# VectorE's small steps taken by turns, seven more pairs of exps for it, and weights loaded at other times, in a fused attention and state-space kernel

## The chip, the cores and the metric

The kernel runs on one core of one Trainium2 chip. The metric is the device time of one execution in microseconds (us), the median of several runs. The core's engines work side by side: TensorE (PE; its weight loads are shown apart as PEld), VectorE (DVE), ScalarE (ACT), GpSimd (POOL), and SyncE (SP), whose queue issues nearly all DMAs here.

## The reference

```python
x = A_x                                         # 1 x 2048 x 1024
g = sigmoid((x * gate_w).sum(-1, keepdims=True))
# a: a diagonal complex state-space model (SSM) of 1024 states over 2048 steps
dt = exp(log_dt); Lam_bar = exp(dt * Lam)
B_bar = ((Lam_bar - 1.0) / Lam)[:, None] * Bmat
Bu = einsum("bld,pd->blp", x + 0j, B_bar)
for t in range(L): h = Lam_bar[None, :] * h + Bu[:, t, :]
a = 2.0 * einsum("blp,dp->bld", hseq, Cmat).real + x * Dskip
# b: attention, 32 heads of 32
q, k, v = (x @ wqkv).reshape(B, S, 3, H, Dh).transpose(2, 0, 3, 1, 4)
p = softmax(einsum("bhqd,bhkd->bhqk", q, k) * Dh ** -0.5)
b = (p @ v).transpose(0, 2, 1, 3).reshape(B, S, D) @ wo
out = g * a + (1 - g) * b
```

## The kernel before

The attention is the frame. Its 32 heads form 8 groups of 4 heads; a group has 8 units (256 queries each), and a unit has 8 bursts (256 keys each): 512 bursts, numbered `p`. In a burst, `burst` puts 8 score matmuls on TensorE (four heads side by side), and two exps, `exp(0)` and `exp(1)`, each over 128 x 1024 scores, turn them into bf16 tiles of `f_pt` (in the first 60 bursts also into other tiles that are still free). Line 1643 is a full exp. One burst later, `pv` (line 1709) multiplies these tiles with V into PSUM bank 6. After a unit, `normalize` takes reciprocals (line 1722) and scales (1723), and a transposing DMA (1729) writes the result to `f_OT`.

**Exps on VectorE.** In chosen bursts one of ScalarE's two exps is short (128 x 768, line 1640): the other 256 columns, one head, are VectorE's. It reads the scores and scales them to integers (line 1633, `x_in`), and for a pair of such bursts runs three steps of a cubic (lines 1667, 1668, 1664, all on the tile `f_xq`); GpSimd then makes bf16 bits of it (1665), and TensorE takes them at line 1688 (`x_pv`), by the end of the unit. `exp(1)` of such a burst waits until `x_in` has read. `X_PLAN` lists the bursts at which a pair starts: a unit has none, one or two. There are 92 pairs.

**Dense work.** Beside the attention, TensorE takes four 512-column matmuls of dense work in a burst, in chains that all gather in PSUM bank 7: the K, V and Q projections of the next group (lines 1426, 1445), the SSM's input u (1457), its output c (1504, with the skip at 1510) and the output projection (1535). The build loop chooses the chains: c if its items are done, otherwise u, otherwise projections, which are forced when the bursts left in the group are few (`left <= need + 4`, where `need` is twice the number of projection chains left). The output chains run last, with ready times from burst 442 on.

**VectorE's background work.** u goes through DRAM (stored at line 1462, reloaded to `f_ub` at 1474) and comes back as 32 *items*, each eleven or so steps: four products with tables, two sums, two scans (1362), two sums to `hp`. Tables and folds of C (`bg2`) are further steps. The loop builds each burst's instruction list with a clock of its own: it adds up the costs written beside each step (`I_MM`, `X_LAST` and others), and fills each burst up to a limit. The steps of exps (`xbg`) come first, then items (`bg`), then `bg2`. Every engine runs its list in order; if a step is later than planned, everything behind it on that engine is late.

**Loads.** B's rows come by transposing DMAs into three slots (1076), C's by `ld_c` (1081) from burst `C_LOADS` = 28, one pair every fourth burst. Projection weights (`ld_w`, line 1071): Q's has one slot, K's and V's two each, so that the weights of group g + 2 are asked for at burst 25 of group g, and Q's of g + 1 at burst 28. The output weights come in five DMAs: two rows at burst 386, six when the c chains are done and later.

**Ending.** For the last unit (queries 1792 to 2047) the output's sums over the first seven groups are made ahead (`part`, `sum7`); two of the four are split in a high and a low bf16 half (lines 1553, 1554) and put into PSUM by four matmuls (`preload`, line 1975) before the last values. After them come the last reciprocal (1984), the scaling (1987), a transpose on TensorE (1990) and four matmuls (2002).

Of the kernel before, what the change touches and what calls it, by code (L numbers as in the profile page):

```python
# [932 lines left out]
C_LOADS = 28  # L933

X_AT = ((0, 2), (4, 6), (0, 4))
X_PLAN = (64, 72, 80, 88, 92, 96, 100, 104, 108, 112, 116, 120, 124, 128, 132, 136, 144, 152, 160, 168, 172, 176, 180, 184, 188, 192, 200, 208, 216, 224, 228, 232, 236, 240, 244, 248, 252, 256, 260, 264, 272, 280, 288, 296, 304, 312, 316, 320, 324, 328, 332, 336, 344, 352, 356, 360, 364, 368, 372, 376, 380, 384, 388, 392, 396, 400, 404, 408, 412, 416, 420, 424, 428, 432, 436, 440, 444, 448, 452, 456, 460, 464, 468, 472, 476, 480, 484, 488, 492, 496, 500, 504)
X_COLS = 256
F_TS, F_ST = 1.32, 1.24
I_MM = 0.61
X_LAST = 0.735  # L940
# [18 lines left out]
class FastPath:  # L959

    def __init__(self, nc, S, es, d, flag):
# [11 lines left out]
        wb = T("wb", [128, 8192], BF)  # L973
        self.wq = wb[:, 0:1024].rearrange("p (a n) -> p a n", a=8)
        self.wkv = wb[:, 1024:5120].rearrange("p (s q a n) -> p s q a n", s=2, q=2, a=8)
        self.bT = wb[:, 5120:8192].rearrange("p (s a n) -> p s a n", s=3, a=8)

        row = lambda o, n: wb[:, o:o + 1024 * n].rearrange("p (a n) -> p a n", a=n)
        self.wo3 = [row(1024, 2), row(5120, 3), row(3072, 1), self.cT[0][:, 0:1, :], self.cT[0][:, 1:2, :]]
        self.wo = [(self.wo3[0][:, a, :], "wo0") for a in range(2)] + [(self.wo3[4][:, 0, :], "wo4")] + [(self.wo3[1][:, a, :], "wo1") for a in range(3)]  # L980
        self.wo += [(self.wo3[3][:, 0, :], "wo3"), (self.wo3[2][:, 0, :], "wo2")]
# [5 lines left out]
        self.hpx = wb[:, 5120:8192].rearrange("p (k n) -> p k n", k=6)  # L987
# [77 lines left out]
    def w_of(self, g, part):  # L1065
        return (self.wkv[:, g % 2, part - 1], ("w", g % 2, part)) if part else (self.wq, ("w", 0, 0))
# [275 lines left out]
    def item_ops(self, j, ch, n):  # L1342
# [9 lines left out]
        def tt(c, o, a, b, op, r, w):  # L1352
            ops.append((c, lambda: dve(lambda e: e.tensor_tensor(o, a, b, op), r, w)))
# [3 lines left out]
        ops.append((0.0, lambda: self.used_u(n)))  # L1357
        tt(0.63, ut[:, 0, :], t[0], t[3], ALU.add, [k[0], k[3]], [("ut", 0)])
# [5 lines left out]
        if ch < 3:  # L1364
            ops.append((0.0, lambda: self.pool(lambda e: e.tensor_copy(self.hl[:, :, j], ht[:, :, 511]), [("ht", 0), ("ht", 1)], [("hl", j)])))
# [368 lines left out]
    def build(self):  # L1734
# [10 lines left out]
        for part in (1, 2):  # L1745
            self.ld_w(1, part)
# [389 lines left out]
```

## Time and profile before

| | |
|---|---|
| median of 3 runs (lowest, highest) | 929.36 us (927.99, 930.2) |
| the profiled execution | 928.11 us |
| its span, first to last instruction | 926.3 us |
| ScalarE busy | 907.3 us (98%) |
| TensorE busy | 902.5 us (97%) |
| VectorE busy | 758.4 us (82%) |
| GpSimd busy | 86.8 us (9%) |
| granted TensorE clock, mean | 0.996 |

Busy times are of one execution. Matmuls are pipelined and their ends modelled, so that TensorE's share says little; its waits say more. Consecutive VectorE and ScalarE instructions overlap a little, so that the distance from start to start, not the busy time of one, is what one costs. The profile also has a timeline, a table of busy time by stage, the waits, and the chain of work that ended last.

### The profile page before, as it was taken

What the parts mean: (1) busy time and instruction counts of PE and PEld (TensorE: products, weight loads), DVE (VectorE), ACT (ScalarE), POOL (GpSimd) and SP (SyncE); (2) the same over time, 40 slices, a digit from 0 to 9 for tenths busy, and PEclk for the clock granted to TensorE, in tenths of its full rate; (3) what the DMA queues carried; (4) which work ended last, traced back from release to release, by engine and by line L of the source; (5) the groups of instructions that cost most, each with busy time, mean ns of one, the idle gap of its engine ahead of it and who ended that gap; (6) DMA issues with size and microseconds to landing.
All of it is one profiled execution on the core that took longest, in us unless ns stands there. A gap on an engine that the chain in (4) does not pass through costs nothing.

```text
span 926.3 us, 33979 instructions
## 1 busy us (share of the span) xinstructions
PE 902.5 (97%) x15316; PEld 503.9 (54%) x15316; DVE 758.4 (82%) x1310; ACT 907.3 (98%) x1034; POOL 86.8 (9%) x156
## 2 busy tenths in 40 slices
PE   8899999999999999999999999999999999999996
PEld 4554754557555565546655565555655655445553
DVE  2788989998989999989989999899988655776665
ACT  6999999999999999999999999999999999999996
POOL 2000000111000101011111020000010010001010
PEclk9999999999999999999999999999999999999998
DMA  9569747750457101272012511413001112424312
GB/s 195 87 116 184 93 84 138 144 116 5 81 113 152 50 20 49 67 147 53 19 51 65 126 45 31 104 63 103 20 15 43 31 51 77 156 83 128 114 62 75
DMA packets 170934, 77.69 MB, mean 84 GB/s; under 512 B 147232, under 2 KB 155424, under 8 KB 170784
## 3 DMA queue, kind: packets, MB, share of 16 engines
q1 hardware_dynamic: 168624, 74.94, 36.3%
q8 instruction: 121, 1.98, 0.9%
q10 hardware_dynamic: 2160, 0.53, 0.3%
q14 instruction: 29, 0.24, 0.1%
HBM read 25.18 MB, written 20.97 MB: 50 GB/s over the span
## 4 chain that ended last, share of the span: by engine, by line
PE 52%; ACT 40%; DVE 4%; DMA 2%; SPq 1%; issue 1%; POOL 0%; DVEq 0%; ACTq 0%
ACT f_pt L1643 32%; PE f_ps L1709 14%; PE f_ps L1624 10%; PE f_ps L1426 9%; PE f_ps L1504 7%; PE f_ps L1457 6%; ACT f_pt L1640 5%; PE f_ps L1445 5%; SPq L1062 1%; ACT f_cT L1643 1%; PE f_ps L1688 1%; DMA f_xT<-in_A_x_dram 1%; ACT f_Et L1643 1%; DMA f_wb<-in_A_B_im_dram 1%; DMA f_ub<-u_scratch 0%
## 5 line engine op out<-in xcount | busy, mean ns | idle before, releaser
L1643 ACT ACTIVATE f_pt<-f_ps 128x1024 bf16<-128x1024 f32 x760 | 728.8, 1090 | 1.5 <-PE f_ps L1624 1.3
L1709 PEld LDWEIGHTS f_ps<-f_V,f_pt 128*128 128x128 bf16 x7184 | 222.2, 96 | 95.3 <-issue 68.7
L1709 PE MATMUL f_ps<-f_V,f_pt 128*128 128x33 bf16 x7184 | 258.0, 178 | 0.0
L1624 PE MATMUL f_ps<-f_Q,f_K 32*128 32x256 bf16 x4096 | 203.3, 273 | 10.8 <-ACT f_pt L1643 3.3
L1640 ACT ACTIVATE f_pt<-f_ps 128x768 bf16<-128x768 f32 x184 | 165.3, 898 | 0.7 <-PE f_ps L1624 0.6
L1624 PEld LDWEIGHTS f_ps<-f_Q,f_K 32*128 32x128 bf16 x4096 | 60.7, 92 | 148.0 <-ACT f_pt L1643 120.6
L1457 PE MATMUL f_ps<-f_xT,f_wb 128*128 128x512 bf16 x512 | 131.5, 379 | 1.6 <-DMA f_wb<-in_A_B_im_dram 0.7
L1665 POOL TENSOR_SCALAR f_xp<-f_xq 128x512 int16<-128x512 f32 x92 | 67.3, 732 | 646.0 <-DVE f_xq L1664 471.3
L1426 PE MATMUL f_ps<-f_xT,f_wb 128*128 128x512 bf16 x464 | 119.3, 379 | 0.1
L1633 DVE TENSOR_SCALAR f_xi<-f_ps 128x256 int32<-128x256 f32 x184 | 77.4, 421 | 17.6 <-PE f_ps L1624 13.3
L1362 DVE TENSOR_TENSOR_SCAN f_ht<-f_pf,f_init,f_ut 128x512 bf16<-128x512 f32 x64 | 81.3, 1279 | 0.0
L1504 PE MATMUL f_ps<-f_cT,f_hp 128*128 128x512 bf16 x272 | 74.5, 379 | 0.1
L1667 DVE SCALAR_TENSOR_TENSOR f_xq<-f_xi 128x512 f32<-128x512 uint16 x92 | 63.7, 692 | 3.2
L1668 DVE SCALAR_TENSOR_TENSOR f_xq<-f_xq,f_xi 128x512 f32<-128x512 f32 x92 | 63.6, 692 | 3.1
L1664 DVE SCALAR_TENSOR_TENSOR f_xq<-f_xi,f_xq 128x512 f32<-128x512 int16 x92 | 63.5, 690 | 2.6
L1457 PEld LDWEIGHTS f_ps<-f_xT,f_wb 128*128 128x128 bf16 x512 | 40.1, 96 | 40.5 <-issue 8.6
L1535 PE MATMUL f_ps<-f_wb,f_OT 128*128 128x512 bf16 x188 | 61.2, 381 | 0.4 <-DVE f_Et L1547 0.4
L1445 PE MATMUL f_ps<-f_wb,f_xT 128*128 128x128 bf16 x896 | 59.3, 219 | 0.0
L1426 PEld LDWEIGHTS f_ps<-f_xT,f_wb 128*128 128x128 bf16 x464 | 36.1, 96 | 35.6 <-issue 7.6
L1461 DVE CAST f_ub<-f_ps 128x512 bf16<-128x512 f32 x64 | 44.1, 688 | 10.4 <-PE f_ps L1457 9.7
L1445 PEld LDWEIGHTS f_ps<-f_wb,f_xT 128*128 128x128 bf16 x896 | 50.4, 97 | 3.8 <-issue 3.8
L1722 DVE RECIPROCAL f_rc<-f_ps 128x8 f32<-128x8 f32 x63 | 13.1, 207 | 47.6 <-PE f_ps L1688 43.5
(149 smaller groups left out, 822.5 us busy)
## 6 DMA issues: line engine op xcount, KB each, us to landing
u_scratch<-f_ub SPq DMA_DIRECT2D x64, 128.0 KB, 2.1
f_ub<-u_scratch SPq DMA_DIRECT2D x32, 256.0 KB, 3.0
ag_scratch<-f_Ag SPq DMA_DIRECT2D x32, 256.0 KB, 2.0
f_hp<-ag_scratch SPq DMA_DIRECT2D x32, 256.0 KB, 3.0
f_wb<-in_B_wqkv_dram SPq DMA_DIRECT2D x21, 256.0 KB, 4.1
out_dram<-f_xT SPq DMA_DIRECT2D x16, 256.0 KB, 2.2
f_OT<-f_On SPq DMA_TRANSPOSE x63, 2.3
f_wb<-in_B_wo_dram SPq DMA_DIRECT2D x1, 768.0 KB
```

The costliest lines, as they stand in the source:

```text
L1362: ops.append((1.24, lambda ri=ri: dve(lambda e: e.tensor_tensor_scan(ht[:, ri, :], rr, ut[:, ri, :], self.init[:, ri, j:j + 1], ALU.mult, ...
L1426: mms.append((1, lambda e, f, l, a=a, w=w: e.matmul(ps[:, bank, :], w[:, a, :], xT[:, a, 512 * ch:512 * (ch + 1)], start=f, stop=l), [tok] ...
L1445: m = e.matmul(ps[:, bank, 128 * q:128 * (q + 1)], xT[:, a, 128 * kt:128 * (kt + 1)], w[:, a, :], start=(a == 0), stop=(a == 7))
L1457: mms.append((1, lambda e, f, l, a=a: e.matmul(ps[:, 7, :], bT[:, (2 * n + ri) % 3, a, :], xT[:, a, 512 * ch:512 * (ch + 1)], start=f, sto ...
L1504: mms.append((1, lambda e, f, l, j=j, ri=ri, h=h: e.matmul(ps[:, 7, :], h[:, cols], cT[ri][:, j, 512 * cb:512 * (cb + 1)], start=f, stop=l ...
L1624: m = e.matmul(ps[:, 2 * sl[h // 2] + h % 2, 256 * kl:256 * (kl + 1)], K[32 * h:32 * h + 32, g % 2, 128 * kt:128 * (kt + 1)], Q[32 * h:32 ...
L1633: first = self.dve(lambda e: e.tensor_scalar(self.xi[:, b % 2, X_COLS * n:X_COLS * (n + 1)], ps[:, 2 * s + 1, 512 - X_COLS:512], X_A, X_LO ...
L1640: self.S.op("act", lambda e: e.activation(flat(self.tile[p]), flat(ps[:, 2 * s:2 * s + 2, :]), ACT.Exp, scale=SCALE), reads=[("S", s)], wr ...
L1643: self.act(lambda e: e.activation(self.tile[p], ps[:, 2 * s:2 * s + 2, :], ACT.Exp, scale=SCALE), [("S", s)], [("pt", p)], "exp")
L1665: self.pool(lambda e: e.tensor_scalar(bits, xq[:], X_K, 128.0 * (E0 + 126.0), ALU.mult, ALU.add), ["xq"], p2, "x_p")
L1667: return [(0.73, 0.0, lambda: self.dve(lambda e: e.scalar_tensor_tensor(xq[:], lo, E2 / E3 * w, lo, ALU.add, ALU.mult), i2, ["xq"], "x_q") ...
L1709: m = e.matmul(ps[:, 6, o:o + 33], self.tile[p][:, h2, 256 * kl + 128 * qt:256 * kl + 128 * (qt + 1)], V[:, g % 2, 2 * i + kl, h, :], star ...
```

## The change

It does the following.

- The background steps carry a second cost, `DEP` = 0.12, counted only if the step follows one of its own kind (*lane*: x for exps, b for items, t for `bg2`). A function `mixed` gives the time of a set of steps taken by turns, and the first lane; the loop puts out one step of that lane and chooses again. The costs themselves are lower.
- `X_PLAN` has seven more entries, 268, 276, 284, 292, 300, 308 and 348: 99 pairs.
- Q's, K's and V's weights have one slot each. K's and V's of the next group are asked for at burst 0 of a group (K's of group 1 at burst 17, V's at the start), Q's at burst 38; the projections may start four bursts after. `C_LOADS` is 32.
- The output weights lie elsewhere and come as eight loads of one row: seven when the c chains are done, the last as before.
- The two steps that split the last sums go to `bg2`. Two of the four preloads come after the last values.

```diff
-C_LOADS = 28
+C_LOADS = 32
+W_AT = (38, 0, 17)
...
-I_MM = 0.61
-X_LAST = 0.735
+DEP = 0.12
+I_MM = 0.6
+X_LAST = 0.615
...
-        tt(0.63, ut[:, 0, :], t[0], t[3], ALU.add, [k[0], k[3]], [("ut", 0)])
-        tt(0.63, ut[:, 1, :], t[1], t[2], ALU.subtract, k[1:3], [("ut", 1)])
+        tt(0.61, ut[:, 0, :], t[0], t[3], ALU.add, [k[0], k[3]], [("ut", 0)], DEP)
+        tt(0.61, ut[:, 1, :], t[1], t[2], ALU.subtract, k[1:3], [("ut", 1)])
...
-                    self.dve(lambda e: e.tensor_copy(hi, su), [("sum7", i)], [("hi", i)])
-                    self.dve(lambda e: e.tensor_tensor(lo, su, hi, ALU.subtract), [("sum7", i), ("hi", i)], [("lo", i)])
+                    self.bg2 += [(0.34, lambda: self.dve(lambda e: e.tensor_copy(hi, su), [("sum7", i)], [("hi", i)])),
+                                 (0.72, lambda: self.dve(lambda e: e.tensor_tensor(lo, su, hi, ALU.subtract), [("sum7", i), ("hi", i)], [("lo", i)]))]
...
+    def mixed(self, xs, bs, ts):
+
+        rest = {"x": list(xs), "b": list(bs), "t": list(ts)}
+        t, lane, lead = 0.0, self.lane, ""
+        while True:
+            some = [s for s in "xbt" if rest[s]]
+            if not some:
+                return t, lead
+            s = next((s for s in some if s != lane), some[0])
+            if rest["b"] and rest["b"][0][0] == 0.0:
+                s = "b"
+            c, d = rest[s].pop(0)
+            lead = lead or s
+            if c > 0:
+                t += c + (d if s == lane else 0.0)
+                lane = s
...
-            if pg == 25 and g + 2 < GROUPS:
-                assert g or not (proj[0] or cur and cur.tag == "proj")
-                for part in (1, 2):
-                    self.ld_w(g + 2, part)
-            if pg == 28 and g + 1 < GROUPS:
-                assert not (cur and cur.tag == "proj")
+            if pg == W_AT[1 if g else 2] and g + 1 < GROUPS:
+                self.ld_w(g + 1, 1)
+                if g:
+                    self.ld_w(g + 1, 2)
+            if pg == W_AT[0] and g + 1 < GROUPS:
+                assert not proj[0]
                 self.ld_w(g + 1, 0)
...
                         for k in range(len(ts) + 1):
-                            u = used_t + sum(ts[:k])
+                            u, lead = self.mixed(xs[:i], bs[:j], ts[:k])
                             if u > room:
                                 break
-                            v = (u + (0.3 * i if ended is not None else 9.0 * i) + 0.05 * sum(bs[:j]), i, j, k)
+                            v = (u + (0.3 * i if ended is not None else 9.0 * i) + 0.05 * sum(x[0] for x in bs[:j]), i, j, k, lead)
...
-        preload()
-        self.pv(4 * NBURST - 4, 4 * NBURST)
+        preload(0)
+        self.pv(4 * NBURST - 4, 4 * NBURST - 2)
+        self.pv(4 * NBURST - 2, 4 * NBURST)
+        preload(1)
```

More of the change, by code (lines that the diff above doesn't have):

```diff
@@ L1806, in build @@
                 if n == 1:
-                    self.xbg += [[c, wait, f] for c, wait, f in self.x_ops(b)]
+                    self.xbg += self.x_ops(b)
+                self.lane = "x"
             q0, q1 = self.quarters[p]
@@ L1838, in build @@
+            if pg == W_AT[0] and g + 1 < GROUPS:
+                assert not proj[0]
                 self.ld_w(g + 1, 0)
             wsv = self.d["B_wo"].rearrange("(a p) n -> p a n", p=128)
-            if p == 386:
-                self.dma(lambda e: e.dma_start(self.wo3[0], wsv[:, 0:2, :]), [], ["wo0"] + [("w", 0, q) for q in (1, 2)], "ld_wo")
-            if not cs and cur is None and not wo1 and self.c_left[3] == 0:
+            if not wo1 and not cs and cur is None and self.c_left[3] == 0:
```

127 lines of the change are left out of this document (64 added, 63 removed).

## Prediction

> **What bounds the kernel now.** I read the page's head first, then ScalarE's waits, then the chain that ended last, then single stretches by the timeline and the table by stage.
>
> ```profile
> span 926.3 us, 33979 instructions
> PE 902.5 (97%) x15316; PEld 503.9 (54%) x15316; DVE 758.4 (82%) x1310; ACT 907.3 (98%) x1034; POOL 86.8 (9%) x156
> ACT f_pt L1643 <- PE f_ps L1624: 1.3, 4, 0.6
> ```
>
> ScalarE is busy for 907.3 of 926.3 us, and its longest sum of waits for scores in the ring of f_pt is 1.3 us. So the exps set the pace almost everywhere, and a change can win in three ways only: fewer columns for ScalarE, fewer of its few stalls, a shorter ending. The profiled execution took 928.11 us, 1.81 over its span; the median of the runs shown is 929.36, or 1.25 above that execution. I make the sum on 928.11 and add the 1.25 at the end.
>
> The chain of waits shows the two paces of ScalarE, for four bursts with one of their eight exps short, and for two bursts with one of four short:
>
> ```profile
> 541.36 6.42 ACT f_pt L1643 x7
> 548.48 6.42 ACT f_pt L1643 x7
> ...
> 839.06 2.75 ACT f_pt L1643 x3
> 842.51 2.75 ACT f_pt L1643 x3
> ```
>
> Four bursts take 548.48 - 541.36 = 7.12 us with one short exp and 2 x 3.45 = 6.90 us with two. A pair is two short exps, so one more pair in a unit of eight bursts brings 2 x 0.22 = 0.44 us: the unit goes from 14.24 to 13.80 us, where ScalarE stays the bound.
>
> TensorE can be the bound instead. In a stretch of c chains with two pairs per unit the chain lies on PE alone; one period of it, from one group of scores to the next:
>
> ```profile
> 739.99 0.33 PE f_ps L1624 x8
> ...
> 741.75 0.33 PE f_ps L1624 x8
> ```
>
> 741.75 - 739.99 = 1.76 us a burst, 14.08 us a unit: more than ScalarE's 13.80. In c chains a second pair is therefore worth 14.24 - 14.08 = 0.16 us, not 0.44.
>
> **The seven added pairs.** They lie at bursts 268, 276, ... 308 and at 348, in units that have one pair now; these begin at 482.5, 496.8, 511.0, 525.2, 539.5, 553.7 and 623.8 us. Which of them are c chains, from the table by stage for line 1504 alone:
>
> ```profile
> 482.50:496.80 14.30, 8.66 (x32) 2.50 (x32) 1.00 0.21 62
> ...
> 511.00:525.20 14.20, 4.34 (x16) 1.25 (x16) 1.00 0.60 141
> 525.20:539.50 14.30, 0.00 (x0) 0.00 (x0) 1.00 0.48 112
> ...
> 623.80:638.00 14.20, 8.67 (x32) 2.50 (x32) 1.00 0.46 118
> ```
>
> The first, the second (a row like the first) and the last are c throughout, the third is half c, the other three hold none. So 3 x 0.16 + 0.5 x (0.16 + 0.44) + 3 x 0.44 = 2.1 us. Bounds: 7 x 0.16 = 1.1 if c chains move there, 7 x 0.44 = 3.1 if they move away.
>
> **VectorE by turns.** A pair costs VectorE two reads of scores and three steps on f_xq. The steps run one behind the other now, beside a pair of item steps that do not need each other, and what VectorE has in one of the stretches to be filled:
>
> ```profile
> 472.69 0.69 DVE L1667 SCALAR_TENSOR_TENSOR f_xq<-f_xi 128x512 f32<-128x512 uint16 x1
> 473.41 0.69 DVE L1668 SCALAR_TENSOR_TENSOR f_xq<-f_xq,f_xi 128x512 f32<-128x512 f32 x1
> 474.14 0.69 DVE L1664 SCALAR_TENSOR_TENSOR f_xq<-f_xi,f_xq 128x512 f32<-128x512 int16 x1
> ...
> 476.19 0.69 DVE L1353 TENSOR_TENSOR f_ht<-f_ub,f_Et 128x1024 bf16<-128x1024 bf16 x1
> 476.80 0.69 DVE L1353 TENSOR_TENSOR f_tq<-f_ub,f_Et 128x1024 bf16<-128x1024 bf16 x1
> ...
> L1633 DVE TENSOR_SCALAR f_xi<-f_ps 128x256 int32<-128x256 f32 x184 | 77.4, 421 | 17.6 <-PE f_ps L1624 13.3
> ...
> 511.00:525.20 14.20, 14.05 (x233) 7.39 (x230) 13.24 (x23) 14.20 (x17) 2.04 (x2) 1.00 0.60 141
> ```
>
> Busy times are alike (0.69), but from start to start a dependent step takes 473.41 - 472.69 = 0.72 us and an independent one 476.80 - 476.19 = 0.61. By turns each dependent step saves 0.11 us: two in each of 99 pairs, three in each of 32 items, together 0.11 x (198 + 96) = 32 us of VectorE, if there is always another step to put between. The seven pairs add 7 x (2 x 0.42 + 3 x 0.61) = 19 us. Over the kernel VectorE ends no fuller than now. The plan's new costs (0.61 and 0.12 on top when dependent, before 0.73) are what these rows show, so the orders it writes should hold on the chip. None of this is itself time: VectorE is not the bound, and I cost it at nothing as long as its reads of scores come before ScalarE needs the bank; the price if that cover goes is the third rival.
> The Trainium skill ("VectorE: DVE Perf Modes", The DRAIN you can't avoid) says that after every operation the pipe empties before the next one starts, and that a chain costs the same with a semaphore after each operation as without. By that rule taking turns would save nothing and the sum would be the third rival's; the trace disagrees, 0.72 against 0.61.
>
> **Q's weights later, C's loads later, K's and V's weights at the unit's start.** Around burst 28 SP's queue carries C, Q's weights and the items' reload in one run:
>
> ```profile
> 65.46 1.29 SPq L1081 DMA_TRANSPOSE f_cT<-in_A_C_re_dram  x1
> ...
> 68.14 1.28 SPq L1071 DMA_DIRECT2D f_wb<-in_B_wqkv_dram  x1
> 69.53 0.67 SPq L1474 DMA_DIRECT2D f_ub<-u_scratch  x1
> ...
> 73.34 0.69 DVE L1353 TENSOR_TENSOR f_ht<-f_ub,f_Et 128x1024 bf16<-128x1024 bf16 x1 [2.39 <-DMA f_ub<-u_scratch]
> ...
> 77.36 1.02 ACT L1643 ACTIVATE f_OT<-f_ps 128x1024 bf16<-128x1024 f32 x1 [1.34 <-PE f_ps L1624]
> ```
>
> The reload is issued at 69.53 behind three issues that began at 65.46; VectorE waits 2.39 us for it, its normalization comes late, and ScalarE stands for 1.34 us. With C's first pair from burst 32 and Q's weights at 38 these three leave its path, up to 69.53 - 65.46 = 4.1 us, more than the 2.39. So I take the 1.34 off; next is VectorE's own work, which ends at 73.34 - 2.39 = 70.95, after the earlier landing at 73.34 - 4.1 = 69.2. Bounds: nothing won, if C's pair at 32 now does the same, to 1.34. The same kind of run costs once more:
>
> ```profile
> 409.55 1.04 PE L1457 MATMUL f_ps<-f_xT,f_wb 128*128 128x512 bf16 x4 [0.69 <-DMA f_wb<-in_A_B_im_dram]
> ...
> 410.97 2.85 ACT L1643 ACTIVATE f_pt<-f_ps 128x1024 bf16<-128x1024 f32 x3 [0.33 <-PE f_ps L1624]
> ```
>
> There a load of B shares the queue and the engines with the weights of bursts 25 and 28 of a group; 0.33 us goes. Against it stand two weight loads right behind the normalization's transpose at each group's first burst, past the stores of u and the loads of B that follow. By the code K's first chain is forced only 28 bursts before the group's end (twice its 12 chains, and 4), that is 36 bursts after the load, so the weights are in time; what can be late is the reload or B. I charge two such events of 0.33 = 0.7 (bounds: none, to one of 1.34 in each of the two groups that start among u chains, 2.7).
>
> **The ending.** The copies of the last sums to two halves run on VectorE right behind their evacuation:
>
> ```profile
> 813.59 2.95 ACT L1643 ACTIVATE f_pt<-f_ps 128x1024 bf16<-128x1024 f32 x3
> 816.65 0.81 ACT L1640 ACTIVATE f_pt<-f_ps 128x768 bf16<-128x768 f32 x1
> ...
> 820.94 2.86 ACT L1643 ACTIVATE f_pt<-f_ps 128x1024 bf16<-128x1024 f32 x3
> ...
> 823.24 0.69 DVE L1554 TENSOR_TENSOR f_Et<-f_Et 128x512 bf16<-128x512 f32 x1
> ...
> 824.36 0.81 ACT L1640 ACTIVATE f_pt<-f_ps 128x768 bf16<-128x768 f32 x1 [0.57 <-PE f_ps L1624]
> ```
>
> Three full exps take 2.75 undisturbed; here 3.06 and 3.42 pass until the short one, which waits for VectorE's read of its scores behind the copy. As background work the copies no longer stand in front of that read: 0.31 + 0.67 = 1.0 us (bounds 0 to 1.0; VectorE has room there, its load falls with the items done). Seven loads of output weights go out together when the last c chain ends, where three did; by the code no output chain starts before burst 442, and the last group's projections lie between, so nothing (four more issues at the reload's 0.67 are 2.7 us of SP's queue, the price if that cover is gone).
> At the very end:
>
> ```profile
> 907.97 9.32 ACT L1643 ACTIVATE f_pt<-f_ps 128x1024 bf16<-128x1024 f32 x10
> ...
> 916.34 1.71 PE f_ps L1975 x4
> 918.04 0.45 PE f_ps L1709 x16
> ...
> 918.52 0.22 DVE f_rc L1984
> ...
> 919.18 0.24 PE f_ps L1990
> ```
>
> The last exp ends at 917.29, but four preloads hold PE until 918.04. With two of them (0.86) behind, the last values end at 916.34 + 0.86 + 0.45 = 917.65, not 918.49: 0.84 earlier. The two moved ones then fill PE until 918.51 and hold back the transpose, due 0.66 after the reciprocal at 918.34, by about 0.2. Gain 0.6 (bounds 0 to 0.84).
>
> **What the reordering may add.** The last step on f_xq hands over to GpSimd, and what runs beside it matters:
>
> ```profile
> 409.51 0.99 POOL L1665 TENSOR_SCALAR f_xp<-f_xq 128x512 int16<-128x512 f32 x1 [9.82 <-DVE f_xq L1664]
> 409.94 1.63 DVE L1362 TENSOR_TENSOR_SCAN f_ht<-f_pf,f_init,f_ut 128x512 bf16<-128x512 f32 x1
> ...
> 470.29 0.27 PE L1688 MATMUL f_ps<-f_V,f_xp 128*128 128x33 bf16 x4 [0.27 <-POOL f_xp L1665]
> ```
>
> A scan beside it takes 1.63 us, and PE once waits 0.27 for its result. Taking turns puts an item's step behind f_xq's last more often. I charge four such waits of 0.27 = 1.1 us, an estimate (bounds 0 to 0.27 for each of 99 pairs, 27, which nothing so far supports).
> The Trainium skill ("SBUF — State Buffer", Who interferes with whom) has a VectorE operation with two SBUF inputs contend with a GpSimd one that reads SBUF, the second blocking fully; the trace agrees in kind (GpSimd's 0.99 and the scan's 1.63 lie over each other). The second rival rests on it.
>
> **Sum.** 2.1 + 1.34 + 0.33 + 1.0 + 0.6 = 5.4 won, 0.7 + 1.1 = 1.8 lost: 3.6 us. 928.1 - 3.6 = 924.5 for such an execution, and 1.25 more for the median: 925.7.
>
> **The rivals.** A measurement of this kernel can tell about 0.2%, 1.9 us, from no change.
> First: the pairs and repairs hold and nothing is lost: 929.36 - 5.4 = 924.0. For it: the units with two pairs run at the undisturbed pace now. It is the good end of the forecast.
> Second, the gain is eaten. GpSimd meets a two-input step in most pairs and PE waits 0.27 for f_xp in twelve more (3.2 us): 925.7 + 3.2 = 928.9, no change. For it: more alternation; against it: f_xp is read some bursts after it is made, and the one wait is 0.27.
> Third, slower: VectorE is overbooked. The place is the stretch from 482 to 568 us, where its row has 13.24 of 14.20 busy, 0.96 free, and each unit gets 2.67 more. If alternating steps still took 0.72, or items found no partner, each of the six units would be 2.67 - 0.96 = 1.71 longer instead of shorter: 6 x 1.71 = 10.3, less 3.3 for repairs and ending, plus 1.8: 929.4 + 8.8 = 938. The point from which it decides: a real spacing near 0.68 (half of the saving lost) is enough to be 4 us worse. For it: the plan fills VectorE with less reserve in each step than before. Against it: the rows have the spacing at 0.61, and steps can move to later units.
> Fourth: the change doesn't fill turns where it matters, the seven pairs bring 1.1, and the weight loads cost their 2.7: 929.4 - 1.1 - (1.34 + 1.0 + 0.6) + 2.7 + 1.1 = 929.2, no change; counted with the second.
>
> **How the numbers follow.** Forecast with the first rival 0.70, all of it faster by over 0.2%; the second and fourth 0.16, no change; the third 0.14, slower. The range takes the first rival and the upper bounds of the pairs (1.0 more), of the ending (0.2) and of the load of B (PE's 0.69 for ScalarE's 0.33, 0.4): 924.0 - 1.6 = 922.4; it goes up over the no-change cases into the mildest third, 931.0. Forecast and first rival alone hold 922.4 to 927.5.
>
> **What would show it.** Right: units from 482 to 568 and at 624 of 13.8 to 14.1 us; f_xq's steps with an item's step between them, 0.61 apart; no idle of 1.34 near 77 us nor of 0.57 near 824; two preloads behind the last values; 198 short exps. Wrong: ScalarE idle in many places behind a late read of scores (line 1633 waiting for nothing), GpSimd's mean far above 0.73 us with PE waiting for f_xp, VectorE waiting for f_ub at a group's start.

## The result, and the profile after

Twelve executions of the kernel after took 926.61 us in the median (925.53 to 927.95), twelve of the kernel before beside them 929.85, so the medians lie 3.2 us apart. The ratio on record, which is not that of the two medians, is 0.9959, 95% interval 0.9944 to 0.9973, or 3.8 us less. The forecast was 925.7 and 3.6 less. In two later series, on two chips, the same kernel gave 0.9973 (0.9960 to 0.9985) and 0.9969 (0.9956 to 0.9982). All three ratios say faster by more than 0.2%, by 2.5 to 3.8 us, though the intervals of the later two reach 0.15 and 0.18%. The profiled execution took 925.63 us.

The head of the page, and the groups of the short exps and of VectorE's reads of scores:

```profile
span 923.9 us, 34036 instructions
PE 901.5 (98%) x15316; PEld 503.1 (54%) x15316; DVE 770.5 (83%) x1345; ACT 905.7 (98%) x1034; POOL 86.4 (9%) x163
...
L1641 ACT ACTIVATE f_pt<-f_ps 128x768 bf16<-128x768 f32 x198 | 176.6, 892 | 0.0
...
L1634 DVE TENSOR_SCALAR f_xi<-f_ps 128x256 int32<-128x256 f32 x198 | 83.4, 421 | 15.9 <-PE f_ps L1625 11.6
```

The 99 pairs are there. VectorE's busy time rose by 12.1 us, ScalarE's fell by 1.6, and ScalarE is still the bound.

For finer reading I cut each span in three, by the starts of the exps: the opening (to the first exp of burst 16), the body (from there to the last exp), the end (from the last exp on). The opening lasts 39.5 to 40.4 us in all profiles here, whichever the kernel. The body of the kernel after is 874.34, 874.29 and 874.30 us in three profiles. I take from this that 0.1 us of body can be read from single profiles; the experiments have one profile each. The end is 9.35 to 10.05 in the same three. The body before is 876.06, the end 10.19. Of the 2.4 us between the two spans shown, 0.55 lies in the opening, 1.72 in the body and 0.14 in the end.

The table by stage for the seven units with a new pair, cut at the starts of their exps (four of the seven shown; columns: stretch, PE, PEld, DVE, ACT, POOL busy, clock, DMA share, GB/s):

```profile
481.50:495.60 14.10, 14.10 (x237) 7.56 (x234) 13.16 (x24) 14.06 (x18) 1.75 (x4) 1.00 0.20 64
495.60:509.50 13.90, 13.87 (x232) 7.35 (x231) 12.95 (x23) 13.90 (x18) 2.26 (x4) 1.00 0.31 83
509.50:523.30 13.80, 13.75 (x230) 7.08 (x227) 13.26 (x23) 13.80 (x18) 1.16 (x3) 1.00 0.77 140
523.30:537.70 14.40, 13.91 (x229) 7.22 (x227) 12.65 (x25) 14.01 (x17) 1.47 (x3) 1.00 0.60 126
...
sum 98.10, PE 97.44 PEld 55.47 DVE 91.29 ACT 97.66 POOL 12.43; mean PE 13.92 PEld 7.92 DVE 13.04 ACT 13.95 POOL 1.78
```

Before, these units took 14.2 to 14.3 us each. Now c chains hold the first at 14.1, with TensorE busy throughout, the next two take 13.9 and 13.8, and one is longer than it was: from 523.3 on, ScalarE has only 14.01 of 14.40 busy. That is the one new loss of size, and it comes in four places. The waits and the timeline of the one at 525 us (start, length, engine and line, then what the engine waited for):

```profile
PE f_ps L1707 <- POOL f_xp L1666: 2.0, 4, 0.6
ACT f_pt L1644 <- PE f_ps L1625: 2.3, 8, 0.6
```

```profile
523.62 0.68 DVE L1354 TENSOR_TENSOR f_tq<-f_ht,f_Et 128x1024 bf16<-128x1024 bf16 x1
524.22 0.69 DVE L1665 SCALAR_TENSOR_TENSOR f_xq<-f_xi,f_xq 128x512 f32<-128x512 int16 x1
...
524.99 0.62 POOL L1666 TENSOR_SCALAR f_xp<-f_xq 128x512 int16<-128x512 f32 x1 [1.95 <-DVE f_xq L1665]
525.66 0.27 PE L1707 MATMUL f_ps<-f_V,f_xp 128*128 128x33 bf16 x4 [0.49 <-POOL f_xp L1666]
...
525.97 0.21 DVE L1741 RECIPROCAL f_rc<-f_ps 128x8 f32<-128x8 f32 x1 [1.07 <-PE f_ps L1707]
...
526.84 0.69 DVE L1462 CAST f_ub<-f_ps 128x512 bf16<-128x512 f32 x1 [0.20 <-PE f_ps L1458]
...
527.18 1.02 ACT L1644 ACTIVATE f_pt<-f_ps 128x1024 bf16<-128x1024 f32 x1 [0.22 <-PE f_ps L1625]
```

By turns, an item's product (L1354) goes in front of f_xq's last step (L1665). The result is due in this very burst: GpSimd is late, TensorE waits 0.49 for f_xp, the reciprocal, the evacuation and the next scores follow late, and ScalarE stands. The units with this (bursts 185, 289, 329, 385) take 0.67, 0.60, 0.76 and 0.66 more than the same unit before, or than a neighbour with two pairs where the unit had one: 2.7 us.

And the turns themselves? In the first of these stretches:

```profile
499.74 0.69 DVE L1668 SCALAR_TENSOR_TENSOR f_xq<-f_xi 128x512 f32<-128x512 uint16 x1
500.46 0.69 DVE L1669 SCALAR_TENSOR_TENSOR f_xq<-f_xq,f_xi 128x512 f32<-128x512 f32 x1
501.19 0.69 DVE L1665 SCALAR_TENSOR_TENSOR f_xq<-f_xi,f_xq 128x512 f32<-128x512 int16 x1
501.80 0.69 DVE L1462 CAST f_ub<-f_ps 128x512 bf16<-128x512 f32 x1
```

The three steps still run one behind the other, 0.72 and 0.73 apart, and only what follows comes after 0.61. Counted over all VectorE instructions, 162 of the 198 successions from one f_xq step to the next are direct (166 of 184 before). Turns are rare.

### The profile page after: what moved, and what is told of

It is laid out like the page before. It is cut to its first block, busy times and chain, and to the rows that moved or that the text cites. A ratio compares the mean times of both kernels' runs of the same rounds, so it can differ in the third digit from the quotient of the medians.

```text
span 923.9 us, 34036 instructions
## 1 busy us (share of the span) xinstructions
PE 901.5 (98%) x15316; PEld 503.1 (54%) x15316; DVE 770.5 (83%) x1345; ACT 905.7 (98%) x1034; POOL 86.4 (9%) x163
## 4 chain that ended last, share of the span: by engine, by line
PE 54%; ACT 36%; DVE 5%; SPq 1%; DMA 1%; issue 1%; POOL 0%; DVEq 0%
ACT f_pt L1644 29%; PE f_ps L1728 14%; PE f_ps L1625 11%; PE f_ps L1427 9%; PE f_ps L1505 8%; PE f_ps L1458 6%; PE f_ps L1446 5%; ACT f_pt L1641 5%; SPq L1063 1%; ACT f_cT L1644 1%; DVE f_ht L1363 1%; ACT f_Et L1644 1%; PE f_ps L1707 1%; DMA f_xT<-in_A_x_dram 1%; PE f_ps L1511 0%
## 5 line engine op out<-in xcount | busy, mean ns | idle before, releaser
L1644 ACT ACTIVATE f_pt<-f_ps 128x1024 bf16<-128x1024 f32 x746 | 718.2, 1086 | 2.7 <-PE f_ps L1625 2.3
L1641 ACT ACTIVATE f_pt<-f_ps 128x768 bf16<-128x768 f32 x198 | 176.6, 892 | 0.0
L1634 DVE TENSOR_SCALAR f_xi<-f_ps 128x256 int32<-128x256 f32 x198 | 83.4, 421 | 15.9 <-PE f_ps L1625 11.6
L1669 DVE SCALAR_TENSOR_TENSOR f_xq<-f_xq,f_xi 128x512 f32<-128x512 f32 x99 | 68.5, 692 | 3.3
L1668 DVE SCALAR_TENSOR_TENSOR f_xq<-f_xi 128x512 f32<-128x512 uint16 x99 | 68.5, 692 | 3.3
L1665 DVE SCALAR_TENSOR_TENSOR f_xq<-f_xi,f_xq 128x512 f32<-128x512 int16 x99 | 68.2, 689 | 2.2
L1536 PE MATMUL f_ps<-f_cT,f_OT 128*128 128x512 bf16 x156 | 44.7, 378 | 0.1
```

What stands on the lines that cost most here:

```text
L1634: first = self.dve(lambda e: e.tensor_scalar(self.xi[:, b % 2, X_COLS * n:X_COLS * (n + 1)], ps[:, 2 * s + 1, 512 - X_COLS:512], X_A, X_LO ...
L1641: self.S.op("act", lambda e: e.activation(flat(self.tile[p]), flat(ps[:, 2 * s:2 * s + 2, :]), ACT.Exp, scale=SCALE), reads=[("S", s)], wr ...
L1644: self.act(lambda e: e.activation(self.tile[p], ps[:, 2 * s:2 * s + 2, :], ACT.Exp, scale=SCALE), [("S", s)], [("pt", p)], "exp")
L1668: return [(0.61, DEP, lambda: self.dve(lambda e: e.scalar_tensor_tensor(xq[:], lo, E2 / E3 * w, lo, ALU.add, ALU.mult), i2, ["xq"], "x_q") ...
L1669: (0.61, DEP, lambda: self.dve(lambda e: e.scalar_tensor_tensor(xq[:], xq[:], E1 / E3 * w * w, lo, ALU.add, ALU.mult), ["xq"] + i2, ["xq"] ...
```

## The experiments

| run | body | end | median us | ratio to before, 95% interval |
|---|---|---|---|---|
| before | 876.06 | 10.19 | 929.85 (beside the first of after) | 1 |
| after, three times | 874.3 | 9.35 to 10.05 | 926.61, 925.67, 926.19 | 0.9959, 0.9973, 0.9969 |
| due step first | 873.48 | 9.60 | 925.23 | 0.9966 (0.9952 to 0.9981) |
| ending undone | 875.27 | 10.18 | 927.9 | 0.9989 (0.9977 to 1.0000) |
| loads at 28 | 874.43 | 9.51 | 926.46 | 0.9973 (0.9958 to 0.9989) |
| 92 pairs | 875.25 | 9.55 | 926.65 | 0.9969 (0.9956 to 0.9983) |
| product held | 873.07 | 9.52 | 924.8 | 0.9953 (0.9938 to 0.9968) |
| no turns, 92 pairs | 876.54 | 9.45 | 927.1 | 0.9977 (0.9963 to 0.9991) |
| no turns, overbooked | 880.06 | 9.77 | 931.98 | 1.0030 (1.0015 to 1.0044) |
| product held longer | 873.61 | 9.30 | 924.9 | 0.9964 (0.9951 to 0.9977) |
| held by place | 872.91 | 10.15 | 924.73 | 0.9953 (0.9938 to 0.9967) |
| no turns, 98 pairs | 874.45 | 9.44 | 925.76 | 0.9974 (0.9963 to 0.9984) |

The kernel before had medians of 927.64 to 930.12 on the chips used, so ratios compare rows better than medians; but most intervals overlap, and where few tenths matter I go by the body. Losses of single units are given against the same unit before, and for burst 289 against a neighbour with two pairs (13.82); the expectations count them from 13.79 throughout.

**Due step first.** The build loop puts f_xq's step first where the pair is due in the next burst:

```diff
+                if best[1] and any(b not in self.x_done for b in self.x_when.get(p + 1, ())):
+                    lead = "x"
```

> The changed kernel with one rule more: if a pair's values are due on TensorE in the next burst, its f_xq step goes first whatever its lane. It swaps two neighbouring VectorE instructions in four places (units 23, 36, 41 and 48) and nothing else. Theory A (taking turns puts an item's step of 0.6 us before a step that is due, and the four stalls of ScalarE of 0.6 to 0.75 us behind line 1707's waits for f_xp come from that): all four go, line 1707 waits for f_xp less than 0.2 us in all instead of 2.0, the units fall from 14.4-14.6 to 13.8-14.1 us, the span from 923.9 to 921.5 or less, the time to 0.993 of before. Rival B (VectorE as a whole is late at these unit starts, or GpSimd is, so that the order of two steps only moves the wait): line 1707 still waits 1.5 us or more in all, the units stay above 14.3 us, the time stays at 0.996.

```profile
523.69 0.68 DVE L1665 SCALAR_TENSOR_TENSOR f_xq<-f_xi,f_xq 128x512 f32<-128x512 int16 x1
...
524.29 0.69 DVE L1354 TENSOR_TENSOR f_tq<-f_ht,f_Et 128x1024 bf16<-128x1024 bf16 x1
524.46 0.99 POOL L1666 TENSOR_SCALAR f_xp<-f_xq 128x512 int16<-128x512 f32 x1 [1.34 <-DVE f_xq L1665]
...
525.51 0.27 PE L1707 MATMUL f_ps<-f_V,f_xp 128*128 128x33 bf16 x4 [0.26 <-POOL f_xp L1666]
```

Half right. All four stalls were to go; they shrank to 0.45, 0.38, 0.42 and 0.44. The step is 0.6 earlier (set against the start of the burst's first full exp, 525.00 here and 524.93 after), but now the product runs beside GpSimd, which takes 0.99 in place of 0.62; f_xp's matmuls come only 0.2 earlier. TensorE's waits for f_xp fell from 2.0 to 1.1 us in sum. The body is 0.8 shorter, not the 2.7 of the stalls.

**Ending undone.** The split of the last sums directly behind their evacuation, and all four preloads ahead of the last values, as before.

```diff
-                    self.bg2 += [(0.34, lambda: self.dve(lambda e: e.tensor_copy(hi, su), ...)),
-                                 (0.72, lambda: self.dve(lambda e: e.tensor_tensor(lo, su, hi, ALU.subtract), ...))]
+                    self.dve(lambda e: e.tensor_copy(hi, su), ...)
+                    self.dve(lambda e: e.tensor_tensor(lo, su, hi, ALU.subtract), ...)
```

> The changed kernel with two parts of its ending undone: the two steps that split a last sum run right behind its evacuation again, and all four preloads stand before the last values. Theory A (each did what the prediction priced): the idle of ScalarE near bursts 454 and 458 is back, about 1.1 us, and the reciprocal of the last unit comes 0.8 us later after the last exp; in all 1.1 us and up to 0.8 more than the changed kernel: span 925.0 to 925.8. Rival B (the ending gains nothing at the last, because the final stores and what follows take up what the reciprocal wins, as the span of the changed kernel suggests, 10.06 us after the start of the last exp against 10.20 before): 1.1 us only, span 925.0, and the stretch from the start of the last exp to the end is the same within 0.2 us.

```profile
822.37 0.69 DVE L1555 TENSOR_TENSOR f_Et<-f_Et 128x512 bf16<-128x512 f32 x1
822.98 0.42 DVE L1634 TENSOR_SCALAR f_xi<-f_ps 128x256 int32<-128x256 f32 x1
```

```profile
823.49 0.81 ACT L1641 ACTIVATE f_pt<-f_ps 128x768 bf16<-128x768 f32 x1 [0.57 <-PE f_ps L1625]
```

The old idle of 0.57 is back, and with it those at bursts 454 and 456; the body is 0.97 longer. The end is 10.18, as before the change, against 9.35 to 10.05. The first part of the ending was worth what the forecast said. Of the second, the last reciprocal does come earlier, as forecast, but how much of it reaches the end varies: the end is 9.30 to 9.77 in ten of the twelve profiles that have this part, and 10.05 and 10.15 in the other two. In the kernel after, the same two kinds of step stand the other way round, the read first:

```profile
817.48 0.42 DVE L1634 TENSOR_SCALAR f_xi<-f_ps 128x256 int32<-128x256 f32 x1
817.83 0.68 DVE L1555 TENSOR_TENSOR f_Et<-f_Et 128x512 bf16<-128x512 f32 x1
```

**Loads at 28.** `C_LOADS = 28`, `W_AT = (28, 0, 17)`: C's first pair and Q's weights again where they were.

> The changed kernel with C's loads from burst 28 and Q's weights at burst 28 of a group again (K's and V's stay at the group's start). Theory A (the 1.35 us at burst 34 and the 0.57 at 222 were SP's queue: C, Q's weights, and K's and V's loads in one run ahead of the items' reload and of B): with two of the three back, VectorE waits for f_ub again in the first group, 1 to 2.4 us, and ScalarE loses 0.5 to 1.35 us near burst 34; near 222 little comes back, as K's and V's loads are not there. Rival B (the stall at 34 went because the items' steps fall elsewhere now that VectorE goes by turns): no wait for f_ub, no loss above 0.2 near burst 34, the same time as the changed kernel.

```profile
65.03 1.29 SPq L1082 DMA_TRANSPOSE f_cT<-in_A_C_re_dram  x1
...
69.01 0.66 SPq L1475 DMA_DIRECT2D f_ub<-u_scratch  x1
...
71.00 1.22 DVE L1336 TENSOR_TENSOR f_OT<-f_OT 128x1024 f32<-128x1024 f32 x1
...
74.57 0.68 DVE L1354 TENSOR_TENSOR f_ht<-f_ub,f_Et 128x1024 bf16<-128x1024 bf16 x1
75.87 1.94 ACT L1644 ACTIVATE f_OT<-f_ps 128x1024 bf16<-128x1024 f32 x2
```

The queue is crowded as before the change, the reload is issued 4 us behind C's first load, and nothing waits for it: VectorE has table steps to do and reaches the item only at 74.57. Before, it stood ready at 70.95. The body differs from the kernel after by 0.1. So the later loads of C and Q do not explain the gain; what took the 1.34 us away is that VectorE's order no longer asks for the reload so early. The two runs without turns have the same order here, so it is not the turns. That the later loads alone, in the order of before, would have done it too was not run, nor were K's and V's weights put back.

**92 pairs.** The kernel after with `X_PLAN` of before.

> The changed kernel with the 92 pairs of before; all else stays. Theory A (a pair is worth 0.44 us where ScalarE is the bound and 0.16 in c chains): the units from 482 to 568 us and at 624 are 14.2 us again, and the span is 2.1 us longer than that of the changed kernel without its stall in unit 36, that is 1.5 us longer with it: about 925.4; ratio to before 0.9975. Rival B (VectorE filled to the brim costs elsewhere what the pairs bring, and the stalls at unit starts come from the pairs): the four stalls of 0.6 to 0.75 us go too, and the span is 923.5 or less.

The body is 0.95 longer, not 2.1, because without the new pairs the steps fall otherwise, and only two stalls of the new kind remain (185 and 377, 0.7 and 0.6, and 0.3 in the unit from burst 320). In the whole time this run (0.9969) can't be told from the kernel after.

**Product held.** Besides the due step going first, the item's product is kept back until the unit's reciprocal and scaling are out:

```diff
+                    hold = self.xbg[0][0] == X_LAST
...
+                if hold and lead != "x":
+                    self.held.append(f)
...
                 self.normalize(q1 // 32 - 1)
+                while self.held:
+                    self.held.pop(0)()
```

> The kernel after, with one rule more: where the last step on f_xq of a pair is due before the next burst's work, it runs ahead of the item's product, and the product is held until the unit's reciprocal and scaling are out. Only four places change, at the bursts 185, 289, 329 and 385. Theory A (order made half of these four stalls, the product beside GpSimd's f_xp the other half): GpSimd's four operations there take 0.62 again, TensorE's wait for f_xp goes from 2.0 us in sum (1.1 with the order alone changed) to 0.3 or less, the four units lose 0.1 to 0.3 in place of 0.73, 0.63, 0.83 and 0.78, the span is 921.3 to 922.0 (923.9 after; 922.9 with the order alone), the median about 924, the ratio to before 0.994 to 0.996. Rival B (the stall is TensorE's own, because any read of f_xp at the last moment stands in the way of the next scores): with GpSimd done earlier the waits for f_xp go, but ScalarE still waits 0.4 to 0.6 at the four places and the span stays at 922.7 or more. Rival C (the held product delays the next reads of scores): VectorE's reads come 0.6 late one burst further on and the stall only moves there.

```profile
525.00 0.62 POOL L1666 TENSOR_SCALAR f_xp<-f_xq 128x512 int16<-128x512 f32 x1 [1.34 <-DVE f_xq L1665]
...
525.98 0.21 DVE L1741 RECIPROCAL f_rc<-f_ps 128x8 f32<-128x8 f32 x1 [1.07 <-PE f_ps L1707]
...
526.57 0.68 DVE L1354 TENSOR_TENSOR f_tq<-f_ht,f_Et 128x1024 bf16<-128x1024 bf16 x1
...
528.21 0.81 PE L1458 MATMUL f_ps<-f_xT,f_wb 128*128 128x512 bf16 x3 [0.42 <-DVE f_xi L1634]
```

GpSimd takes 0.62 again and TensorE waits for f_xp nowhere: the waits view has no such line. That confirms the second half of the cause. But rival C came true as well: the product now stands in front of the next read of scores, and TensorE waits 0.42 for that. The four units still lose 0.35, 0.31, 0.35 and 0.48, more than the 0.1 to 0.3 expected.

**Product held longer,** behind the next read of scores.

```diff
+            elif self.held:
+                while self.held:
+                    self.held.pop(0)()
```

> As in the run where the item's product was held until the unit's scaling was out, but held one burst's reads longer: in the four places it now comes behind the evacuation of the dense chain and behind VectorE's next read of scores. In that earlier run GpSimd's result was in time, the reciprocal came 0.44 us behind its burst's first exp (1.04 in the kernel after), and then the held product stood 0.6 in front of the evacuation and the read, so that ScalarE still lost 0.32 to 0.39 at the burst behind. Theory A (the whole stall is VectorE's order; what is left is the place of that one product): the read comes 0.5 to 0.6 earlier, the four units lose 0.1 to 0.2 each (0.73, 0.63, 0.83, 0.78 after; 0.41, 0.34, 0.41, 0.60 with the shorter hold), the last exp begins about 1.0 us earlier than with the shorter hold, 912.5 to 912.9, the span is 921.7 to 922.3 and the median about 923.5. Rival B (the burst behind a unit loses 0.3 in any order, because reciprocal and scaling themselves stand in front of the evacuation): the losses stay at 0.3 to 0.4 each and the span at 922.8 or more.

> The kernel after itself, on the same chip as the run with the product held longer, so that the two can be set against one another. Theory A: 1.5 to 2.0 us slower than that one, four stalls of 0.6 to 0.8 in the same four places. Rival: no difference in the times beyond 0.5 us, since the opening varies by that much from run to run.

Three places are mostly mended (units of 14.22, 14.05, 14.06 us for 14.52, 14.42, 14.61), but the fourth, at 385, takes 15.22 for 14.57: no dense chain ends there, VectorE stood idle until the read, and three item steps were pushed behind it. The medians on that chip are 0.77 us apart in favour of this run, half of what was expected.

**Held by place.** As the last one, but where no chain ends, the product goes right behind the scaling.

```diff
+            while self.held and ended is None:
+                late = True
+                self.held.pop(0)()
```

> The run with the product held behind the next read of scores, with one exception: at burst 385, where no dense chain ends and VectorE stood 0.6 us idle behind the scaling, the product goes right behind the scaling and the next product behind the read. Elsewhere (185, 289, 329) as in that run. Theory A (three of the four places were mended there, and the 1.43 us of the fourth came from three item steps pushed behind the read of burst 386 and then the evacuation of 388): unit 48 loses 0.2 to 0.6 in place of 1.43, the other three 0.26 to 0.43 as in that run, the last exp begins 0.8 to 1.2 us earlier, near 912.7, the span is 921.7 to 922.3, the median near 923.9, 1.5 us or more below the kernel after on the same chip. Rival B (the stall at 388 comes from the c chain's own evacuation and not from the item steps): unit 48 still loses over 1.0 and the span stays at 922.9.

> The kernel after once more, as the measure on this chip for the run beside it. Theory A: 1.5 to 2.0 us slower than that run; rival B: about 0.8 slower, as against the version before it.

```profile
525.45 0.21 DVE L1741 RECIPROCAL f_rc<-f_ps 128x8 f32<-128x8 f32 x1 [1.07 <-PE f_ps L1707]
...
526.92 0.41 DVE L1634 TENSOR_SCALAR f_xi<-f_ps 128x256 int32<-128x256 f32 x1
527.26 0.68 DVE L1354 TENSOR_TENSOR f_tq<-f_ht,f_Et 128x1024 bf16<-128x1024 bf16 x1
...
527.73 0.93 ACT L1641 ACTIVATE f_pt<-f_ps 128x768 bf16<-128x768 f32 x1
```

The read stands in front of the product and ScalarE goes on without a gap. The body is 1.4 us shorter than after's; the median is 924.73 (924.20 to 925.19) against 926.19 (925.24 to 928.01) on the same chip: 1.46 less. It has the shortest body here, though only 0.16 shorter than with the product held until the scaling is out. The unit at 385 takes 14.61, so it is not mended: at 698.65 us, in burst 388, TensorE waits 0.72 for VectorE's read of scores, which comes behind the pair's steps and the evacuation of the c chain; which of these made it late was not separated.

**No turns, 92 pairs.** In `mixed`, `s = some[0]`: exps' steps first, then items, then tables, with the dependent step still counted 0.12 longer.

> The kernel after with the pairs of before (92), and VectorE's steps not by turns but as before: steps of exps first, then items, then tables (the added cost of a dependent step is counted as in the kernel after, so the order that is written is no fuller than VectorE). Loads and ending stay as in the kernel after. Theory A (turns are no time by themselves, they only make room for pairs, and they cost the stalls at the first burst behind a unit where an item's product got in front of the last step on f_xq): against the run with 92 pairs by turns (span 924.9) the stalls at 185 and 377 go, GpSimd finds no item's step in front of it, and the span is 924.0 to 924.6. About burst 34: the reload of u is used earlier again when items are not held back by table steps, but it is also issued earlier, 65 instead of 69.5 us, behind fewer loads; so VectorE waits under 1 us for it and ScalarE less than 0.4. Rival B (turns are worth something of their own, because the reads of scores come earlier when VectorE has more free time): stalls on late reads appear in many places, VectorE's wait for scores falls below 17 us in sum, and the span is above 925.5.

Against 92 pairs by turns the body is 1.29 longer. Of this, 1.13 is one wait for a load of B at burst 70, which the run with 98 pairs does not have though its steps are the same up to there, so it is no matter of the order. The other 0.16 is what turns are worth at equal pairs, a balance of single units 0.2 to 0.35 longer or shorter. Nor are the stalls theirs alone, which theory A had: those at 185 and 377 are there without turns too, 0.45 and 0.38, and an item's product runs beside GpSimd there (0.99 and 1.00), as in the first experiment.

**No turns, overbooked.** The same order with 99 pairs and `DEP = 0.0`: the plan takes a dependent step for 0.61.

> The kernel after with its 99 pairs and all its costs, but the steps not by turns (exps, then items, then tables), and a dependent step booked at its 0.61 alone, so that the order that is written takes VectorE to be faster than it is: what the third rival said, made true on purpose. From the traces a dependent step takes 0.72. Theory A (third rival's price): in the full stretches VectorE falls behind by 0.11 for each dependent step, reads of scores come late, and each of the six units with new pairs between 482 and 568 us becomes up to 1.7 us longer than before instead of 0.1 to 0.4 shorter; with the repairs kept the span is 930 to 936 against 923.9. Rival B (slack takes it): VectorE has some 120 us free over the kernel and waits for scores at each read, so it catches up within a unit, the loss is only a few stalls of 0.3 to 0.7, and the span is 924.5 to 927.

```profile
PE f_ps L1458 <- DVE f_xi L1634: 4.0, 14, 0.6
```

```profile
577.66 0.41 DVE L1634 TENSOR_SCALAR f_xi<-f_ps 128x256 int32<-128x256 f32 x1
...
578.11 0.81 PE L1458 MATMUL f_ps<-f_xT,f_wb 128*128 128x512 bf16 x3 [0.48 <-DVE f_xi L1634]
...
579.30 2.85 ACT L1644 ACTIVATE f_pt<-f_ps 128x1024 bf16<-128x1024 f32 x3 [0.20 <-PE f_ps L1625]
```

This is the third rival's case, an overbooked VectorE, and it is slower than before. In u's chains TensorE now waits 14 times for a read of scores, 4.0 us in sum; in the three profiles of the kernel after it does so never, never and four times (1.2). But the 5.7 us of body more than the kernel after are spread over some twenty units, 0.2 to 0.8 in each; the six units from 482 to 568 us take 85.1 together, against 83.9 after and 85.4 before.

**No turns, 98 pairs.** The order of the run with 92, costs as in the kernel after, and six of the seven pairs (348 finds no room).

> The kernel after without turns (exps' steps, then items, then tables; a dependent step still counted with 0.12 more), and with six of the seven added pairs: all but 348, which finds no room. In the trace of the kernel after, f_xq's three steps run right behind one another in 162 of 198 places (166 of 184 before), so turns are rare there. Theory A (turns are next to no part of the gain; the pairs are, and they need only the plan's other costs): against the run without turns and with 92 pairs (last exp begins at 916.49, of which 1.13 is one late load of B at burst 70 that need not come back) the six pairs bring 1.5 to 2.1 and no unit pays for the missing turns, so the last exp begins at 913.3 to 915.0 and the median is within 1 us of the kernel after, 925.5 to 927. Rival B (turns carry it: without them VectorE is fuller and its reads of scores come late in the units with two pairs from 482 to 568 us): these six units do not get below 14.2 us, VectorE's wait before its reads of scores falls to 10 us or less in sum, or the last exp begins at 916 or later, and the median is 928 or more.

```profile
DVE f_xi L1634 <- PE f_ps L1625: 13.0, 29, 1.0
```

The body is 0.15 longer than after's, and VectorE waits as long for scores (13.0; 11.6 after). The turns are not where the gain comes from. They are not the only source of late steps either: TensorE waits five times for f_xp here, 0.25 to 0.33 each. What made room for the pairs was not tested. It may be the costs, booked by what runs ahead of a step, or the weights' new places; no run has the kernel before with nothing but the seven pairs added, and with C's and Q's loads back at 28 all 99 still fit.

## Why the prediction came out right, and where its steps were wrong

**Pairs (2.1).** The seven units are 2.2 shorter, one stall of 0.60 set aside: 0.13, 0.34, 0.39, 0.42, 0.42, 0.41 and 0.07. Reading the two limits (ScalarE 0.44, TensorE in c chains 0.16) off the trace of before held in the main; each unit got slightly less. That the sum fits so well has some luck in it, for the c chains moved. From the table by stage for line 1505 alone, the second unit has 8 matmuls of c left of 32, and the third none:

```profile
495.60:509.50 13.90, 2.16 (x8) 0.63 (x8) 1.00 0.31 83
509.50:523.30 13.80, 0.00 (x0) 0.00 (x0) 1.00 0.77 140
```

With these, the prediction's own limits give 2 x 0.16 + 0.37 + 4 x 0.44 = 2.45 in place of 2.1. Taken out of the kernel after, the seven pairs are worth 0.95 of body, because stalls come and go with them.

**The ending (1.0 and 0.6).** 1.14 won at bursts 454 to 458, 1.16 lost again at the same bursts when the part was undone. At the end the last reciprocal comes 0.45 behind the end of the last exp, where it was 1.23 before:

```profile
912.27 2.76 ACT f_pt L1644 x3
...
915.48 0.22 DVE f_rc L2005
```

Counted from the last exp's start it comes after 1.63, 1.82 and 1.63 in the three profiles of the kernel after, 2.41 before and 2.37 with the part undone: 0.6 to 0.8 earlier, near the forecast (0.84 without what the moved preloads take back). The end is 0.1 to 0.8 shorter, 0.5 in the mean of three.

**The stall at 77 us (1.34).** Gone by 1.35, and yet this step failed: the loads were named as the cause, and the run with C's and Q's loads at their old places has no stall either. The reload was late only as measured by VectorE's early request for it; the order of VectorE's steps removed the request. The step left out that a wait has two ends. The 0.57 at burst 222 went too (forecast 0.33), and so did 0.40 at 257 that I had not charged; what removed these two was not separated.

**What reordering adds (1.1).** The right kind of place, the wrong mechanism, and too small. GpSimd is slowed less often, not more: over 0.9 us are 18 of its 92 operations before and 9 of 99 after, and its mean fell from 732 to 676 ns, as the groups of the two pages show:

```profile
L1665 POOL TENSOR_SCALAR f_xp<-f_xq 128x512 int16<-128x512 f32 x92 | 67.3, 732 | 646.0 <-DVE f_xq L1664 471.3
```

```profile
L1666 POOL TENSOR_SCALAR f_xp<-f_xq 128x512 int16<-128x512 f32 x99 | 66.9, 676 | 618.9 <-DVE f_xq L1665 418.5
```

What costs is an item's product ahead of a step that is due at once: four stalls of 0.60 to 0.76, 2.7 us, where four of 0.27 were charged. The four waits of TensorE for f_xp are there, but of 0.49 to 0.56 each, and the reciprocal and the evacuation behind them add to that. The Trainium skill ("SBUF — State Buffer", Who interferes with whom) bears on the first experiment; it has a VectorE operation with two SBUF inputs contend with a GpSimd one that reads SBUF. With the due step ahead, GpSimd's operation took 0.99 beside the product, which has two inputs, and 0.62 without it, so the trace agrees.

**Weight loads (0.7).** No wait at a group's start in the kernel after: 0. The kind of event that was charged does exist: the 1.13 at burst 70 in the run with 92 pairs and no turns is a wait for a load of B issued behind K's and V's weights. In place of the 0.7 stand small losses that the sum did not have, 0.30, 0.22 and 0.30 in the units of bursts 28, 40 and 58 and about 0.1 or less in others, 1.2 us in sum with the small gains set against them. In the three large ones no load is waited for; TensorE waits 0.16 to 0.26 for VectorE's evacuation of the dense chain before, as here:

```profile
63.06 1.02 PE L1458 MATMUL f_ps<-f_xT,f_wb 128*128 128x512 bf16 x4 [0.25 <-DVE f_ub L1462]
```

What makes the evacuation late I did not separate.

**Turns (costed at nothing).** The 32 us of VectorE time that they were to save were mis-sized by far: direct successions of dependent steps went from 228 to 212, of f_xq's from 166 to 162 and of items' from 62 to 50 of 96. At 0.11 each that is about 2 us, and VectorE is 12.1 us busier, where the prediction had it no fuller. Before the change, too, 52 of the 280 were not direct, so there was less to save than the prediction took. That f_xq's step costs 0.73 behind its own predecessor and 0.61 otherwise was right, and the overbooked run shows the price of ignoring it, a body 5.6 longer than without turns at 98 pairs. The prediction held against this a rule of the Trainium skill ("VectorE: DVE Perf Modes", The DRAIN you can't avoid), but left out how that paragraph ends: a next operation that is not held back starts earlier. The trace agrees with that end, since behind a step of 0.69 the next follows after 0.61 if it needs nothing from it.

**The sum.** In the body 2.2 + 1.35 + 0.57 + 0.4 + 1.14 = 5.66 won, 2.7 + 1.2 lost: 1.8, where the two bodies differ by 1.76; with 0.5 at the end 2.3. The medians of the three series differ by 2.0 to 3.9, the ratios say 2.5 to 3.8. What is over 2.3 lies in the opening, which varies by itself, or is not in these profiles; its cause stays open. So the forecast's 3.6 is at the upper side. That it lies within the measured ones is partly luck: the prediction had the wrong cause for a gain, a loss 1.6 too small, another of 0.7 that did not come, one of 1.2 and two gains of 0.2 and 0.4 that it did not see, and these partly cancelled.

**The rivals.** The fourth, that the change does not do what it says, is true for the turns but not for the time. The third's point held (late reads), its price did not: overbooked, the kernel came out 2.7 us above before rather than 8.8, and not where the rival put it.

## What to carry to other kernels

A stall put down to a late transfer has two ends: see when the consumer would next have asked for it, and test the load alone before crediting it. When steps are reordered to save time on an engine that is not the bound, look first for the step that is due at once; one product of 0.6 us ahead of it cost more than a pair of exps brings (0.44), and setting three of those four places mostly right took 1.4 us more off the body. And count in the trace how often the new order really occurs before believing that it is what helped.

## What the hardware showed that I had not expected

GpSimd's 128x512 conversion took 0.62 us alone and 0.99 to 1.00 beside a bf16 product of 128x1024 on VectorE, so putting the product behind the due step brought only 0.2 of the 0.6 us. VectorE's steps of 0.69 busy follow one another after 0.61 if independent and after 0.73 if not, in the median of each profile here. The body of the kernel after repeats within 0.05 us in three profiles, two of them from chips of their own, while over all profiles the opening (39.5 to 40.4) and the end with its new order (9.30 to 10.15) vary by nearly 1 us each.
